# Attending the first batch in two halves of four heads

## The chip, the cores and the metric

One core of a Trainium2 chip runs the whole program. The metric is the device time of one execution in microseconds. Kernels that are compared ran alternately on the same chip. The kernel before took 986.52 us (median of 4 runs, 986.08 to 986.72).

## The reference, cut to what matters

```python
# attention, B, H, S, D = 8, 8, 576, 64
q_p, k_p = phi(q), phi(k)            # relu(x)*cos, relu(x)*sin, side by side: 128 features
kv  = einsum('bhsf,bhsd->bhfd', k_p, v);  z = k_p.sum(2)
num = einsum('bhsf,bhfd->bhsd', q_p, kv)
den = einsum('bhsf,bhf->bhs', q_p, z)[..., None] + 1e-6
x   = (num / den).transpose(0, 2, 1, 3).reshape(4608, 512)
# mixture of 8 experts, gates balanced by 8 rounds of row and column scaling over all tokens
out = sum_e P[:, e] * (relu(x @ w1[e]) @ w2[e])      # 512 -> 1024 -> 512
```

Each batch gives 576 tokens. The FFN walks through nine blocks of 512 tokens, so block 0 needs only batch 0, block 1 needs batches 0 and 1, and so on.

## The kernel before: the parts that matter

In this kernel TensorE (`te`), VectorE (`ve`) and ScalarE (`se`) each run their instructions in the order in which the program writes them: the helper below ties every call to the one before. A wait in one place therefore delays all that follows on that engine.

```python
class InOrder:                        # every call is tied to the one before on its engine
    def __getattr__(self, name):
        def call(*args, **kwargs):
            i = getattr(self.engine, name)(*args, **kwargs)
            not_before(self.last, i)
            ...

def keep_busy(n):                     # "fillers": products of ones, the result is not used
    for _ in range(n):
        te.matmul(out=idle_ps[:, 0:P], lhsT=ones_sq[:], rhs=ones_sq[:], start=True, stop=True)
```

The first batch is handled whole: queries, keys, values, sums, one set of denominators for all eight heads, with fillers in TensorE's waits. Then its four tiles of two heads each are attended; beside them the keys and values of batch 1 are prepared, and the first sixteen FFN products (four per tile) begin as soon as a tile is there.

```python
load(0, 0, "q"); ...; load(0, 1, "q")
for name in "kv": load(0, 0, name); load(0, 1, name)
...
for hk in range(HK):                  # q_p on VectorE, transposed on TensorE, moved by ScalarE
    prep_q(0, hk); ...turn(0, hk, i, True)
for hk in range(HK):
    prep_k(0, hk); prep_kp(0, hk)
keep_busy(16)
for half in range(2):
    prep_v(...); prep_v(...)
    begun.append(sums_begun(0, half))
    keep_busy((4, 6)[half])
sums_made(0, 0, begun[0]); sums_made(0, 1, begun[1])
epsilons(0)
denominators(0)                       # 24 products, then reciprocal, cast, remainder on VectorE
keep_busy(34)
...
for hk in range(HK):
    attend(0, hk)
    prep_k(1, hk); prep_kp(1, hk)     # keys of batch 1
    if hk >= 2: prep_v(1, hk - 2, se.copy)
    for kt in ((), (0,), (1,), (2, 3))[hk]:
        ...                           # four 512-wide FFN products for tile kt
```

The rest of batch 1 is placed into the 16 slots of block 0 (eight of the first FFN layer, eight half tiles of the second), and the start of batch 2 into its last slots:

```python
at(0, 4, prep_q, 1, 0); at(0, 4, ...sums_begun(1, 0)); at(0, 5, ...sums_made(1, 0)); ...
at(0, 8, denominators, 1)
at(0, 11 + hk, attend, 1, hk)
...
(11, prep_k, 0), (11, prep_q, 0), (12, prep_k, 1), (12, prep_kp, 0), ... # batch 2, block 0's slots
```

From batch 2 on the queries are transposed by a transfer, not by TensorE.

The softmax here doesn't subtract the row's maximum and nothing guards it: scores larger than these inputs give would overflow.

## Time and profile before

| | kernel before |
|---|---|
| time, us (median) | 986.52 |
| TensorE busy, share of the span | 98% |
| half clock after the start, us | 15.7 to 22.5 |
| first FFN product / last of the first sixteen ends, us | 25.1 / 30.5 |
| denominators of batch 1 end, us | 40.8 |
| block 1 starts / its gates start, us | 50.3 / 58.8 |

The page says where to look: after the start TensorE is nearly full. From 25 to 75 us it idles 1.6 us in all, from 75 to 175 us not at all, and its later waits (3.4 us between 175 and 225 us, some 6 us in the 760 us after that) are not touched by this change. Only the start can be won or lost. There the milestones of the last rows are read from the timeline of TensorE (first product of a kind, with its start). The prediction shows the lines.

### The profile page before, as it was taken

How to read it: one execution, taken by the hardware profiler on the slowest of the kernel's cores; microseconds unless marked ns; L12 is line 12 of the kernel's file. 1: busy time of each engine (PE TensorE's matmuls, PEld its weight loads, DVE VectorE, ACT ScalarE, POOL GpSimd, SP SyncE). 2: the span in 40 equal slices, each digit the busy share in tenths (PEclk: the TensorE clock that was granted, in tenths of full speed). 3: DMA queues.
4: the chain of work that ended last, by engine and by line, in shares of the span. 5: the costliest groups of instructions: out<-in, count | busy, mean ns of one | idle time of the engine just before them, and what ended most of it. 6: DMA issues, size and time to landing. Idle time of an engine off the chain costs nothing.

```text
span 984.8 us, 20226 instructions
## 1 busy us (share of the span) xinstructions
PE 969.9 (98%) x7844; PEld 678.4 (69%) x7844; DVE 805.8 (82%) x1830; ACT 568.6 (58%) x1269; POOL 60.6 (6%) x82
## 2 busy tenths in 40 slices
PE   8999999989999999999999999999999999999997
PEld 7545444447777777777777777777777777777775
DVE  5786774789889888988789888988888888988887
ACT  5776665467776555555555555555555555555551
POOL 6311110010000000000000000000000000000001
PEclk8999999999999999999999999999999999999999
DMA  9989990741013410133103400233103401104435
GB/s 162 206 122 162 157 151 9 136 77 47 34 41 68 85 32 25 49 68 68 49 25 69 91 25 25 56 62 67 49 25 68 92 25 27 47 26 117 128 87 129
DMA packets 80336, 73.54 MB, mean 75 GB/s; under 512 B 33264, under 2 KB 72176, under 8 KB 80240
## 3 DMA queue, kind: packets, MB, share of 16 engines
q0 software_dynamic: 27232, 30.94, 20.0%
q1 hardware_dynamic: 52768, 41.06, 17.2%
q8 instruction: 61, 1.00, 0.4%
q14 instruction: 35, 0.29, 0.1%
q10 hardware_dynamic: 240, 0.26, 0.1%
HBM read 83.12 MB, written 12.98 MB: 98 GB/s over the span
## 4 chain that ended last, share of the span: by engine, by line
PE 94%; DVE 2%; DMA 2%; ACT 1%; POOL 1%; issue 0%; POOLq 0%; ACTq 0%; SPq 0%
PE rows_ps L109 34%; PE h_ps L109 28%; PE copied_ps L109 11%; PE p_ps L109 11%; PE y_ps L109 6%; PE small_ps L109 4%; DMA v_ld<-in_v_dram 1%; DMA q_pT<-q_p 0%; DVE acc_hi L847 0%; POOL hs_last L862 0%; DVE P_tok L109 0%; DMA out_dram<-acc_lo 0%; DVE colp L109 0%; ACT u L109 0%; POOL k_ld L201 0%
## 5 line engine op out<-in xcount | busy, mean ns | idle before, releaser
L847 DVE SCALAR_TENSOR_TENSOR acc_lo<-rows_ps,P_tok,acc_lo 128x512 f32<-128x512 f32 (+1 forms) x322 | 203.1, 639 | 74.8 <-PE rows_ps L109 74.7
L109 PEld LDWEIGHTS <-H 128*128 128x128 f16 x2080 | 203.0, 98 | 83.1 <-issue 1.2
L783 ACT CAST u<-h_ps 128x384 f16<-128x384 f32 x288 | 137.6, 478 | 130.7 <-PE h_ps L109 130.7
L109 PEld LDWEIGHTS <-w1e 128*128 128x128 f16 x1632 | 156.4, 98 | 66.2 <-issue 6.0
L777 DVE CUSTOM_DVE_ANT_0 H<-p_ps,u 128x384 f16<-128x384 f32 x329 | 180.9, 550 | 6.7 <-PE p_ps L109 6.6
L109 PEld LDWEIGHTS <-hs 128*128 128x128 f16 x1500 | 146.6, 98 | 56.2
L109 PE MATMUL h_ps<-S,w1e 128*128 128x384 f16 x672 | 164.1, 326 | 1.1 <-ACT u L109 0.9
L109 PE MATMUL p_ps<-xT,T 128*128 128x384 f16 x672 | 164.1, 326 | 0.1
L109 PE MATMUL rows_ps<-V,H 128*128 128x256 f16 x1000 | 150.0, 273 | 0.7 <-DVE acc_hi L847 0.7
L109 PE MATMUL h_ps<-xT,w1e 128*128 128x384 f16 (+1 forms) x616 | 150.1, 350 | 0.2 <-DVE xT L109 0.2
L109 PE MATMUL rows_ps<-w2e,hs 128*128 128x256 f16 x1000 | 150.0, 273 | 0.0
L815 ACT ACTIVATE H<-h_ps 128x384 f16<-128x384 f32 x144 | 70.6, 490 | 95.1 <-PE h_ps L109 95.1
L109 PEld LDWEIGHTS <-T 128*128 128x128 f16 x1008 | 98.1, 98 | 29.5 <-issue 3.1
L109 PE MATMUL rows_ps<-w2e,H 128*128 128x256 f16 (+1 forms) x568 | 91.2, 285 | 0.0
L796 ACT COPY copied_ps<-h_ps 128x384 f32<-128x384 f32 x144 | 67.5, 469 | 36.0 <-PE h_ps L109 35.2
L806 ACT ACTIVATE H<-copied_ps 128x384 f16<-128x384 f32 x144 | 70.8, 492 | 20.4 <-PE copied_ps L109 20.4
L109 PE MATMUL h_ps<-S,T 128*128 128x384 f16 x336 | 81.8, 325 | 0.4 <-ACT copied_ps L109 0.3
L109 PE MATMUL copied_ps<-xT,w1e 128*128 128x384 f16 x336 | 82.1, 326 | 0.0
L109 PE MATMUL copied_ps<-w2e,H 128*128 128x256 f16 x504 | 75.5, 272 | 0.0
L109 PE MATMUL rows_ps<-V,hs 128*128 128x256 f16 x500 | 74.9, 272 | 0.0
L847 DVE SCALAR_TENSOR_TENSOR acc_lo<-copied_ps,P_tok,acc_lo 128x256 f32<-128x256 f32 x126 | 60.0, 476 | 0.4
L847 DVE SCALAR_TENSOR_TENSOR acc_hi<-rows_ps,P_tok,acc_hi 128x512 f32<-128x512 f32 (+1 forms) x56 | 41.3, 737 | 20.6 <-PE rows_ps L109 19.7
(140 smaller groups left out, 956.9 us busy)
## 6 DMA issues: line engine op xcount, KB each, us to landing
S<-x_saved SPq DMA_DIRECT2D x108, 192.0 KB, 2.4
out_dram<-acc_lo SPq DMA_DIRECT2D x62, 128.0 KB, 2.4
w1e<-in_moe_w_dram POOLq DMA_DIRECT2D x7, 1024.0 KB, 9.0
w2e<-in_moe_w_dram POOLq DMA_DIRECT2D x7, 1024.0 KB, 9.6
q_ld<-in_q_dram POOLq DMA_DIRECT2D x16, 288.0 KB, 7.4
k_ld<-in_k_dram POOLq DMA_DIRECT2D x16, 288.0 KB, 8.3
v_ld<-in_v_dram POOLq DMA_DIRECT2D x16, 288.0 KB, 9.4
x_saved<-S SPq DMA_DIRECT2D x18, 192.0 KB, 1.9
```

Of the source, the lines that this page charges most:

```text
L109: i = getattr(self.engine, name)(*args, **kwargs)
L777: latest = ve._custom_dve(TENSOR_ADD_SAT, out=out, in0=ps[:, 0:TU], in1=t[:], s0=FP32_MAX, s1=0.0)
L783: se.copy(out=t[:], in_=ps[:, 0:TU])
L796: se.copy(out=Y[:, 0:TU], in_=X[:, 0:TU])
L806: se.activation(out=h11, in_=Y[:, 0:TU], func=AF.Relu)
L815: se.activation(out=h12, in_=X[:, 0:TU], func=AF.Relu)
L847: ve.scalar_tensor_tensor(out=a, in0=rows, scalar=P_tok[:, g, self.e : self.e + 1], in1=a, op0=ALU.mult, op1=ALU.add,)
```

## The change

Its intent is to have the FFN products start sooner. The loads bring queries, keys and values of the first four heads ahead of the others. These heads get sums, denominators, a reciprocal chain (reciprocal, cast, remainder) and two attends of their own, so the first FFN products start while the other four heads still come in. The second half pays for its own denominators and reciprocals. In exchange, most fillers go (46 of the 60 between the parts of the batch), the weights of the first layer are loaded whole before batch 1, batch 1 is prepared later (slots 4 to 8 of block 0), batch 2 one slot later, and block 0's second layer first runs the half sums of all four tiles, two of them in PSUM tiles of the first layer.

```diff
-        load(0, 1, "q")
-        for name in "kv":
-            load(0, 0, name)
-            load(0, 1, name)
+        load(0, 0, "kv")
+        load(0, 1)
...
-        keep_busy(16)
-        for half in range(2):
-            prep_v(...)
-            begun.append(sums_begun(0, half))
-            keep_busy((4, 6)[half])
-        sums_made(0, 0, begun[0])
-        sums_made(0, 1, begun[1])
-        epsilons(0)
-        denominators(0)
-        keep_busy(34)
-        ... four attends, each with prep_k(1), prep_kp(1), prep_v(1) and FFN products
+        keep_busy(14)
+        ... prep_v(0, 0), prep_v(0, 1)
+        begin(0, 0)
+        epsilons(0)
+        made(0, 0)
+        prep_q(0, 2)
+        denominators(0, range(4))
+        turn_all(0, 2, True)
+        prep_k(0, 2)
+        prep_q(0, 3)
+        attend(0, 0)
+        prep_k(0, 3)
+        prep_v(0, 2, se.copy)
+        prep_kp(0, 2)
+        turn_all(0, 3)
+        prep_v(0, 3, se.copy)
+        attend(0, 1)
+        prep_kp(0, 3)
+        first(0)
+        begin(0, 1)
+        epsilons(0)
+        made(0, 1)
+        first(1)
+        denominators(0, range(4, 8))
+        attend(0, 2)
+        attend(0, 3)
+        first(2)
+        first(3)
...
+                for half in range(2):
+                    for hk in (2 * half, 2 * half + 1):
+                        at(0, 4 + half, prep_k, 1, hk, False)
+                        at(0, 4 + half, prep_kp, 1, hk)
+                        at(0, 4 + half, prep_v, 1, hk, se.copy)
+                at(0, 5, begin, 1, 0)
+                ... queries in slots 6 and 7, transposes in 7 and 8
-                    at(0, 11 + hk, attend, 1, hk)
+                    at(0, (10, 12, 13, 14)[hk], attend, 1, hk)
...
-                    (11, prep_k, 0), (11, prep_q, 0), (12, prep_k, 1), (12, prep_kp, 0), ...
+                    (12, prep_k, 0), (12, prep_q, 0), (13, prep_k, 1), (13, prep_kp, 0), ...
...
-                    if j == 0 and slot < FT + 4:
-                        ts, part = part, ts
+                    if j == 0:
+                        part, ts = divmod(slot - FT, TCH // P)
```

## The prediction

> **What bounds the kernel now.** I read the page first, then a table of stretches of the first 61 us, the timeline of TensorE, VectorE and ScalarE there, and the chain of work that ended last between 25 and 61 us.
>
> ```profile
> PE 969.9 (98%) x7844; PEld 678.4 (69%) x7844; DVE 805.8 (82%) x1830; ACT 568.6 (58%) x1269; POOL 60.6 (6%) x82
> PE 94%; DVE 2%; DMA 2%; ACT 1%; POOL 1%; issue 0%; POOLq 0%; ACTq 0%; SPq 0%
> ```
>
> TensorE is busy for 98% of the span and is 94% of the chain that ended last. The change touches only what happens before the second of nine token blocks (block 1) begins, so it can be worth only what TensorE loses there to waits, fillers and a low clock.
>
> ```profile
> 12.40:15.70 3.30, 1.05 (x41) 0.91 (x40) 2.38 (x5) 1.91 (x4) 1.54 (x3) 1.00 1.34 198
> 15.70:19.10 3.40, 3.40 (x61) 2.31 (x62) 0.73 (x5) 1.15 (x5) 2.08 (x3) 0.50 1.27 205
> 19.10:22.50 3.40, 3.40 (x44) 3.08 (x39) 2.08 (x3) 0.00 (x0) 1.43 (x2) 0.50 1.23 205
> 25.00:31.00 6.00, 5.80 (x36) 2.50 (x35) 5.82 (x12) 5.62 (x14) 2.85 (x4) 1.00 1.23 206
> 31.00:41.00 10.00, 9.08 (x153) 5.73 (x152) 6.05 (x15) 7.08 (x17) 5.15 (x8) 1.00 1.22 206
> 41.00:51.00 10.00, 10.00 (x76) 4.97 (x75) 7.95 (x18) 7.51 (x18) 0.56 (x1) 1.00 1.23 201
> ```
>
> Columns: stretch, length, busy time (and count) of PE, PEld, DVE, ACT, POOL, then granted clock, DMA share, GB/s. TensorE has 1.05 us of work between 12.4 and 15.7, and then runs at half clock until 22.5. Between 25 and 31 us VectorE (5.82 of 6) and ScalarE (5.62 of 6) are full: that is the attention of batch 0 with the keys of batch 1 prepared beside it. The transfers run at some 200 GB/s throughout.
>
> ```profile
> 14.60 1.03 PE L109 MATMUL small_ps<-acc_lo,k_p 64*128 64x65 f16 x36 [2.13 <-ACT acc_lo L109]
> 20.13 3.19 PE L109 MATMUL y_ps<-ones_sq 128*128 128x128 f16 x34
> 23.16 0.41 PE L109 MATMUL small_ps<-hl,acc_hi 96*128 96x192 f16 x3
> ```
>
> TensorE waited 2.13 us for values (all loads before them being first), then filled with 34 products of ones while VectorE made reciprocals. The first FFN product is at 25.1 us, the last of the sixteen "first" ones ends at 30.5.
>
> ```profile
> 34.04 0.23 DVE zsel L109
> 36.66 0.67 DVE q_p L109
> 37.33 0.93 DVE q_pT L109 x2
> 38.26 0.66 DVE q_p L109
> 39.39 1.00 DVE acc_hi L109 x2
> 40.76 0.97 PE y_ps L109 x4
> 50.50 1.74 PE h_ps L109 x8
> 54.39 4.09 DMA q_pT<-q_p
> ```
>
> This is the chain: after the first FFN products, the path is the preparation of batch 1 on VectorE and ScalarE up to its denominators (end 40.76); after that TensorE is dense and block 1 starts at 50.5. So two numbers decide: when the denominators of batch 1 are done, and what follows.
>
> [...] In the trace the loads land one after another, a 288 KB load per 1.43 us (counted from the packets), so a new order moves landings but not their sum.
>
> **The change part by part.**
>
> 1. Loads. Positions in the queue are served as seen by first users at 5.99, 8.45, 10.12, 13.03, 13.88 and 15.37 us. Before: both q, both k, both v halves. After: q, k, v of four heads, then of the others. The first values arrive at 10.12 instead of 13.88. w1 follows whole (about 16.7 to 20.6), then batch 1 (k, v by 26, q by 29), w2 by 34.5: none late for its user.
>
> 2. First half. VectorE: two q_p to 7.4, then two k (0.31+0.76 each) from 8.45 to 10.7. ScalarE: six transposed tiles to 10.4 (12 took 4.71 us before), two value copies (1.25) to 11.7. Sums end near 12.3 instead of 17.26. zsel (0.39), 12 denominator products: 13.1. But q_p of tile 2 stands in front of the reciprocal: 13.03 to 13.78. Then reciprocal 1.35, cast 0.31, hl 0.41: 15.9 instead of 22.4. Gain here 6.5 us.
>
> 3. Between the halves. attend(0) needs rb copies (0.70) and multiplications (0.82): 17.7. Then tile 3: relu of k (0.70), two value copies (0.66 each), k_p (0.76), two evictions on VectorE (0.55 each) and a third on ScalarE, all in front of attend(1), whose PSUM tiles come from the same four: xT 1 at 20.8, k_p 3 at 21.5, sums at 22.0.
>
> 4. Second half. It pays its own denominator: 23.6; a second VectorE chain of 1.35+0.31+0.41 = 2.07 us: 25.7. attend(2) 27.45, attend(3) 28.5, and the last first product 29.5, against 30.5. So of the 6.5 us only 1.0 is left: the second half comes through the same VectorE.
>
> 5. Clock. TensorE loses 46 of the 60 fillers between the batch's parts. Work of about 1.3 us from 12.4 to 15.7 is like the 1.05 of before, so I expect half clock from 15.7 here too, now under attend(0), tile 3 and the first FFN products. Half clock adds about 0.4 us to attend(0)'s two groups, 0.3 to attend(1), 0.4 in the sums: about 1.1 us, which takes the gain of 1.0.
>
> 6. Batch 1. Before, its relu, k_p and values were made in the full stretch from 25 to 31. After, they come behind it: VectorE does four relu (0.31) and four k_p (0.76), 28.5 to 32.8, and the four value copies stand between the evictions of hT on ScalarE: from 28.9 four hT 2.16, fifth 0.55, two values 1.25, hT 0.60, two values 1.25, kv_sb 0.43 gives 35.15; zsel 0.2 later: 35.35. Here VectorE was idle for two microseconds. Then on VectorE, in order: two q_p 1.5, eviction 0.55, zsel (behind kv_sb of the second half on ScalarE) 38.25, q_p 0.75, two evictions 1.0, q_p 0.75, three evictions 1.6: 42.35. Denominators of batch 1 end at 42.65, against 40.76.
>
> 7. From there to block 1 the work is that of before (seven half tiles of FFN2, the gates, four attends): 50.5 - 40.76 = 9.7 us. Taking all four first halves first lets attend(0) stand after the third half tile; its hl is ready 2.45 us after the denominators (0.35+1.35+0.30+0.41 and gaps), the work in front is 2.15: a stall of 0.3 at most.
>
> Sum: block 1 starts near 52.4 with full clock and 53.4 with half clock in between, instead of 50.5: +1.9 to +2.9 us. Afterwards TensorE is dense until 175 us, so the difference stays. A hand schedule with so many waits is good to perhaps 2.5 us, and the placing of the slots looks as if it had been tuned on the chip, which speaks for less; I take +1.5 us: 988.2.
>
> **Rivals.**
>
> A. The intended gain arrives: first FFN products at 20 us instead of 25.1, fillers of 3.19 us gone, and batch 1 catches up in the FFN slots because its loads have landed. For it: before, VectorE worked 30.9 of 45 us between 6 and 51, so there is room for the added 2.07. Against it: the room lies in waits of a serial chain. It would give 982.5 to 985.
>
> B. Half clock bites twice: [...]attend(2), attend(3) and eight large products (0.86 us more per four) run slow. +4 to +5 us: 991.
>
> C. Transfers hide everything: the landing of batch 2 sets block 1. Against: by packets batch 2 is in by 42 us, and the one wait in block 1 is 0.5 us, for a transpose that took 4.09 us while loads ran. If block 1 came 3 us earlier this wait would grow by perhaps 1 us and eat a third of A's gain. If it comes later, nothing changes.
>
> **Range and chances.** A at about 35% puts the time at 983 to 986.5, my schedule at 987.5 to 989.7 has about half, B the rest. The range is 984.3 to 991.3. Two per cent is 19.7 us, twice all that TensorE loses before block 1 (about 10 us from 14.6 on), so beyond 2% is nearly excluded: faster 0.01, same 0.98, slower 0.01.
>
> **What would show it.** Right: first hl near 16, second near 25.7; the last first product within a microsecond of 30; zsel of batch 1 waiting for kv_sb on ScalarE past 34.5; its denominators at 42 to 44; block 1 at 52 to 54; half clock from about 15.7[...]. Wrong: denominators of batch 1 before 40.7, or block 1 before 50; TensorE dense from 20 us on; full clock throughout. If block 1 starts earlier by some microseconds but the end doesn't follow, rival C was right.

## More of the kernel before

In the trace of the kernel before VectorE waits 2.84 us for the sums of batch 1, and the queries written after them start behind it, at 34.35 us.

## The result, and the profile after

The changed kernel took 995.69 us (median of 4 runs, 992.33 to 997.21) against 986.52. The ratio is 1.0089, with a 95% interval from 1.0062 to 1.0116; ratios are the mean time of one kernel's fast runs over that of the other's of the same rounds, so not quite the ratio of the medians. That is within 2%, as forecast, but 9.2 us slower and outside the predicted range. The runs also spread over 5 us, where those of before lie within 0.7 us. Their granted clocks sort them, but not all of the loss is in the mean clock: the run at 0.997, the mean clock of the kernel before in its profiled run, is still 5.8 us over.

```text
run      997.21  996.34  995.04  992.33 us
clock    0.990   0.990   0.991   0.997      (mean of the run)
```

The clock row of the page, 40 slices of 24.6 us before and 24.9 us after, shows a second dark slice. First before, then after:

```profile
PEclk8999999999999999999999999999999999999999
```

```profile
PEclk8899999999999999999999999999999999999999
...
PE 93%; DVE 3%; ACT 2%; DMA 1%; issue 0%; POOL 0%; ACTq 0%; SPq 0%; POOLq 0%
```

Here is the table of stretches after the change, in lengths of 3.4 us, cut where the clock changed. Half clock lasted 3.4, 6.8, 10.2, 13.7, 17.1 and 23.9 us in the profiled runs told of here, each close to a multiple of 3.4; one expectation below calls such a length a window. The columns are as in the prediction: after the busy times comes the granted clock.

```profile
12.50:15.90 3.40, 1.87 (x31) 1.12 (x28) 3.33 (x6) 2.46 (x7) 1.80 (x3) 1.00 1.37 198
15.90:19.30 3.40, 2.98 (x21) 1.75 (x18) 2.85 (x7) 3.16 (x8) 1.71 (x3) 0.50 1.43 199
19.30:22.70 3.40, 3.40 (x47) 1.55 (x46) 1.41 (x5) 0.43 (x2) 1.88 (x3) 0.50 1.21 206
22.70:26.20 3.50, 2.60 (x19) 0.84 (x16) 0.85 (x1) 0.00 (x0) 1.45 (x3) 0.50 1.21 207
26.20:29.60 3.40, 1.86 (x12) 0.80 (x13) 2.04 (x5) 0.80 (x3) 1.70 (x3) 0.50 1.22 205
29.60:33.00 3.40, 3.40 (x12) 1.28 (x12) 2.90 (x8) 0.91 (x3) 0.44 (x1) 0.50 1.24 206
33.00:36.40 3.40, 2.71 (x29) 1.24 (x28) 2.03 (x5) 3.40 (x8) 1.43 (x2) 1.00 1.21 206
```

Half clock lasted from 15.9 to 33.0 us: 17.1 us instead of 6.8. Under it lay the first sixteen FFN products, but for the end of the last, and the second half of the batch. The timeline shows what the intent was, that it arrived, and what it became:

```profile
18.95 1.03 PE L109 MATMUL h_ps<-xT,w1e 128*128 128x512 f16 x2
27.74 0.66 PE L109 MATMUL small_ps<-hl,acc_hi 96*128 96x192 f16 x3 [2.44 <-DVE hl L109]
32.87 0.66 PE L109 MATMUL y_ps<-xT,w1e 128*128 128x512 f16 x2
38.19 0.39 DVE L109 TENSOR_TENSOR zsel<-acc_hi,small_ps 128x64 f16<-128x64 f16 x2 [3.08 <-ACT kv_sb L109]
45.70 1.04 PE L109 MATMUL y_ps<-w2e,hT 128*128 128x512 f16 x4
66.10 0.34 PE L109 MATMUL small_ps<-q_pT,zsel 128*32 128x192 f16 x6 [1.42 <-DMA q_pT<-q_p]
66.89 3.37 PE L109 MATMUL h_ps<-xT,w1e 128*128 128x512 f16 x8
```

And the same waits in the kernel before (the first from its list of waits between 20 and 45 us: us in total, times, longest; the wait in question is the longest):

```profile
DVE zsel L109 <- ACT kv_sb L109: 3.5, 2, 2.8
58.52 0.35 PE L109 MATMUL small_ps<-q_pT,zsel 128*32 128x192 f16 x6 [0.52 <-DMA q_pT<-q_p]
59.31 1.89 PE L109 MATMUL h_ps<-xT,w1e 128*128 128x512 f16 x8
```

The first FFN product starts 6.2 us earlier than before. Then TensorE waits 2.44 us for the second reciprocal chain, and the last of the first sixteen ends at 33.5 us, 3.0 us later than before. VectorE sits idle for 3.08 us until ScalarE has moved the sums of batch 1; that wait was there before (2.84 us), but it now ends 4.2 us later. The denominators of batch 1 end at 45.8, 5.0 us later than before, and block 1 starts at 55.7. In block 1 there is a longer wait for a transpose, 1.42 us instead of 0.52, and after it eight products take 3.37 us instead of 1.89: the clock was lost once more, from 67.1 to 70.5 us. The gates of block 1 start at 66.4 (+7.6) and those of block 2 at 87.7 (+9.3). After that the kernels run alike, but for another 1.4 us by the end of this profiled run, the slowest of the four.

The chain of waits after the change has pieces that are new or longer (the piece of the transpose was 4.09 us before, that of the eight products 1.75):

```profile
25.35 1.36 DVE den L109
32.68 1.77 ACT hT L109 x4
35.64 0.72 ACT acc_lo L109
61.14 4.92 DMA q_pT<-q_p
67.03 3.23 PE h_ps L109 x8
```

The second reciprocal, the evictions of hT with the value copies of batch 1 among them, a transpose of batch 2, and slow products: each is a candidate, and the experiments take them one by one.

### The profile page after: what moved, and what is told of

Its sections match the earlier page's. It is cut to its first block, busy times and chain, and to the rows that moved or that the text cites.

```text
span 995.5 us, 20149 instructions
## 1 busy us (share of the span) xinstructions
PE 973.6 (98%) x7804; PEld 675.8 (68%) x7804; DVE 809.4 (81%) x1840; ACT 567.5 (57%) x1267; POOL 59.0 (6%) x80
## 4 chain that ended last, share of the span: by engine, by line
PE 93%; DVE 3%; ACT 2%; DMA 1%; issue 0%; POOL 0%; ACTq 0%; SPq 0%; POOLq 0%
PE rows_ps L109 33%; PE h_ps L109 28%; PE copied_ps L109 11%; PE p_ps L109 11%; PE y_ps L109 5%; PE small_ps L109 4%; ACT acc_lo L109 1%; DMA q_pT<-q_p 0%; DVE den L109 0%; ACT hT L109 0%; ACT q_pT L109 0%; DVE acc_hi L887 0%; ACT k_ld L109 0%; POOL hs_last L902 0%; DVE P_tok L109 0%
## 5 line engine op out<-in xcount | busy, mean ns | idle before, releaser
L109 PEld LDWEIGHTS <-w1e 128*128 128x128 f16 x1632 | 157.3, 98 | 69.6 <-issue 10.7
L109 PE MATMUL h_ps<-xT,w1e 128*128 128x384 f16 (+1 forms) x616 | 153.4, 356 | 0.3 <-DVE xT L109 0.3
L109 PEld LDWEIGHTS <-T 128*128 128x128 f16 x1008 | 98.1, 98 | 29.5 <-issue 3.1
## 6 DMA issues: line engine op xcount, KB each, us to landing
w2e<-in_moe_w_dram POOLq DMA_DIRECT2D x7, 1024.0 KB, 10.2
```

## The experiments

Three theories. **Clock**: the fillers that were taken out had kept the clock, and most of the loss is half clock. **Chain**: the order of work on VectorE and ScalarE (batch 1 late, values in front of evictions) makes the loss, and the clock only follows. **Slots**: what is lost inside block 1 comes from putting batch 2 one slot later. A fourth question came up on the way: what stands behind these.

"Over before" in the text is the median minus the median of the kernel before in the same rounds; it drifts by some tenths of a us from one set of rounds to another.

### Fillers put back, nothing else

```diff
-        keep_busy(14)
+        keep_busy(24)                      # before the values
...
         turn_all(0, 2, True)
+        keep_busy(20)                      # before attend(0)
...
         denominators(0, range(4, 8))
+        fill(30)                           # the same into a fresh PSUM tile: before attend(2)
```

> The changed kernel with products of ones put into the three waits of TensorE in the first batch: 24 instead of 14 before the values, 20 more before attend(0), 30 before attend(2); nothing else moves. Clock theory (the loss beyond 2 to 3 us is half clock, which came because the fillers were taken out): half clock falls from the 17 us of the changed kernel's profile to 7 us or none, no second half-clock stretch in block 1, first FFN products end near 30 us instead of 33.5, time 989 to 991.5 and runs within 1 us of each other. Chain theory (the loss is the order of work on VectorE and ScalarE, and the clock only follows): under 1.5 us gained, 994 to 996.

Measured: 989.22 us (988.23 to 989.98), ratio 1.0027 [1.0012, 1.0042]. 6.5 us of the 9.2 are gone. The same stretches with fillers:

```profile
19.30:22.70 3.40, 3.26 (x62) 1.50 (x59) 1.50 (x5) 0.43 (x2) 1.51 (x3) 1.00 1.22 207
22.70:26.20 3.50, 2.76 (x44) 2.18 (x39) 2.32 (x4) 0.60 (x2) 2.12 (x3) 1.00 1.21 206
26.20:29.60 3.40, 3.23 (x18) 1.42 (x18) 3.08 (x8) 1.88 (x6) 1.43 (x2) 1.00 1.23 206
```

The clock stays full until 38.6 us, and the first products end at 29.1 instead of 33.5. In the profiled run one stretch of 3.4 us was left, from 38.6 on, under the denominators of batch 1. The runs lie within 1.8 us, where the clock theory expected 1. It holds for the larger part. 2.7 us over before are left for the others.

### Which of the fillers

```diff
 a_fill1: keep_busy(24), keep_busy(20), no fill(30)
 a_fill2: keep_busy(14), no keep_busy(20), fill(30)
```

> The changed kernel with only the early fillers (24 before the values, 20 before attend(0)), none in the wait for the second reciprocal. If the early waits lose the clock and the dense products then hold it: close to the kernel with all fillers, 989 to 991, half clock at most one stretch of 3.4 us. If the wait of 2.4 us for the second reciprocal is enough to lose it by itself: half clock from about 26 us under the last eight first products, 991.5 to 994.

> The changed kernel with only the fillers in the wait for the second reciprocal. The clock is then lost at about 16 us as before, and the fillers bring it back one or two windows earlier than in the changed kernel (33 us): half clock 7 to 12 us, 990.5 to 993. If the early loss decides: 994 to 996, no gain.

Measured: 991.12 us (990.61 to 991.72) with the early ones alone, 992.54 us (990.17 to 992.9) with the late ones alone; over before 5.2 and 6.7. Neither is enough. In the profile with early fillers the clock is lost in the wait for the second reciprocal, without an earlier loss:

```profile
23.50:26.90 3.40, 1.37 (x12) 0.82 (x13) 2.38 (x5) 1.05 (x3) 1.87 (x3) 1.00 1.21 206
26.90:30.30 3.40, 3.40 (x11) 1.16 (x9) 3.03 (x8) 0.92 (x4) 1.71 (x3) 0.51 1.23 206
```

The first stretch has 1.37 us of work; after it comes half clock, under the last of the first products. With the late ones alone, half clock lasted from 13.7 to 27.4 us in the profiled run. So the change made two places in which the clock is lost, and the second one is new: it is the second reciprocal chain.

### The same fillers taken from the kernel before

```diff
-        keep_busy(16)
+        keep_busy(14)
...
-            keep_busy((4, 6)[half])
...
         denominators(0)
-        keep_busy(34)
```

> The kernel before with its fillers reduced to the 14 that the changed kernel keeps (16, 4, 6 and 34 become 14, 0, 0 and 0). Clock theory: the half-clock stretch lengthens from 6.8 us to 10 to 17 us and reaches the first FFN products, time 988.5 to 992, and the runs spread by more than 1 us. Chain theory: the fillers stood in waits anyway and nothing moves, 986 to 987.5.

Measured: 987.46 us (985.79 to 990.08), over before 0.9, ratio 1.0012 [0.9995, 1.003]: not clear of nothing, but with a spread of 4.3 us. The expectation of the clock theory was too high. In the profiled run half clock lasted 10.2 us, from 15.4 to 25.6, and the time was 985.79: no loss at all in that run. TensorE was busy for 7.8 of the 10.2 us, with sums, denominators and the first attends, and it waited 2.2 us for the reciprocal chain, but only the first four FFN products lay there; the first one started at 24.3, before the 25.1 of the kernel with fillers. There the 34 fillers, at half clock, end at 23.3 us, though the reciprocal chain is done at 22.4. So taking out fillers need not cost anything by itself. That half clock costs most where dense products and a serial chain lie under it, and that the change put both there, is a reading of these traces and was not tested apart.

### Batch 1 earlier in the changed kernel

```diff
         made(0, 1)
+        for hk in (0, 1): prep_k(1, hk); prep_kp(1, hk)
+        for hk in (0, 1): prep_v(1, hk, se.copy)
         first(1)
...      # and of the keys and values in slots 4 and 5 only the other two tiles' stay, in slot 5
-                at(0, 5, begin, 1, 0); at(0, 5, made, 1, 0)
+                at(0, 4, begin, 1, 0); at(0, 4, made, 1, 0)
```

> The changed kernel with keys and values of the first four heads of batch 1 prepared in the idle stretch of VectorE and ScalarE before the second reciprocal, and their sums one slot earlier. Chain theory: denominators of batch 1 end 2 to 3 us earlier than the 45.8 us of the changed kernel, block 1 starts 2 to 3 us earlier, time 992.5 to 994 with the half clock left as it is. Clock theory: the start of block 1 is set by the half-clock first products, under 1 us gained.

Measured: 996.08 us (995.43 to 996.5), no gain; the expectation of the chain theory failed. The denominators of batch 1 end at 45.9 us, as without the edit. VectorE now waited 5.1 us for the sums of batch 1 on ScalarE, then made the other two tiles' keys, and only then the queries. Half of the work was earlier, but the end of the line was not.

### Late batch 1 alone, in the kernel before

```diff
         for hk in range(HK):
             attend(0, hk)
-            prep_k(1, hk); prep_kp(1, hk); prep_v(...)
...
+ slots 4 to 8 of block 0 filled with batch 1 as in the changed kernel
```

> The kernel before with one part of the change alone: batch 1 prepared in slots 4 to 8 of block 0 as in the changed kernel, everything else and all fillers as before. The prediction's step 6 (late preparation costs 1.9 us): denominators of batch 1 near 42.5 us, 988 to 989.5. If VectorE and ScalarE, now unburdened during the attends, give it back: the first FFN products end 1 us or more earlier and the time is 986 to 987.5.

Measured: 988.37 us (988.27 to 989.78), ratio 1.003 [1.0018, 1.0043], over before 2.5. From the chain of waits of this kernel:

```profile
36.96 0.39 DVE zsel L109 x2
39.02 1.71 PE y_ps L109 x4
40.73 1.93 PE small_ps L109 x25
```

The denominators of batch 1 end at 42.66 us, 1.9 us later than before, though the first FFN products end at 29.0, 1.5 us earlier. The number is that of the prediction's step 6, but the late preparation is only a part of it. The second `zsel` pair, at 36.96 us, is 0.7 us later than before (36.27). The stretch before 38.6 us then has 2.05 us of TensorE work in 3.40, and from 38.6 to 42.0 us the clock is half once more: four products of the second layer take 1.71 us of the chain instead of 0.97. The remaining 1.2 us were lost there.

Two pairs of traces agree. The kernel with all fillers (`a_fill`) and the one with fillers and the old slots (`a_fill_slots`, below) are the same program up to slot 10 of block 0, and only the first has half clock from 38.6 to 42.0: its denominators end at 42.8 us, against 41.7. `a_fill_slots` and the first of the mended kernels (`a_best`, below) both keep the clock in their profiled runs and differ only in late or early preparation: 41.7 against 40.9 us, with medians 0.5 us apart and ranges that overlap. So late preparation by itself costs some 0.7 us at the denominators. What else lies in the 2.5 us was not separated.

### The order of the second layer alone, in the kernel before

```diff
-                    if j == 0 and slot < FT + 4:
-                        ts, part = part, ts
+                    if j == 0:
+                        part, ts = divmod(slot - FT, TCH // P)      # PSUM of two tiles from ps_h
...
-                    at(0, 11 + hk, attend, 1, hk)
+                    at(0, (10, 12, 13, 14)[hk], attend, 1, hk)
```

> The kernel before with one part of the change alone: block 0 runs the first halves of all four tiles up front, two of them in the PSUM tiles of the first FFN layer, with the attends of batch 1 at the changed slots. All theories say that this part is neutral: 986 to 987. If holding the PSUM tiles into block 1 costs something, 987.5 to 989.

Measured: 987.54 us (985.63 to 988.58), ratio 1.0012 [1.0, 1.0025]: at the edge of being clear, over before 1.6 by medians. In the trace attend(0) of batch 1 now comes before its reciprocal is there:

```profile
43.49 0.42 PE L109 MATMUL small_ps<-hl,acc_hi 96*128 96x192 f16 x3 [0.34 <-DVE hl L109]
```

and from the denominators of batch 1 to the gates of block 1 it takes 19.1 us instead of 18.0. The stall is 0.34 of that. For the rest, the trace shows ScalarE's rb copies and evictions bunched, so that PSUM comes free later; that is a reading of it, and the order and the slots of the attends were not tested apart. The part is not neutral, as I had expected; it costs about 1 us by the trace.

### The old slots for batch 2, without and with fillers

```diff
-                    (12, prep_k, 0), (12, prep_q, 0), (13, prep_k, 1), (13, prep_kp, 0), ...
+                    (11, prep_k, 0), (11, prep_q, 0), (12, prep_k, 1), (12, prep_kp, 0), ...
```

> The changed kernel with the preparation of batch 2 put back to the slots of before (11 to 15 instead of 12 to 15). If the late slots cause the loss inside block 1 (4 us there in the profile): the wait for the last transpose falls from 1.4 us to 0.5 or less, the half-clock stretch at 67 us goes, and the time falls by 2 to 4 us to 992 to 994. If the slots don't matter (VectorE is late for other reasons): within 1 us of the changed kernel.

> The changed kernel with both the fillers of the first experiment (989.2 us) and the old slots for batch 2 (993.3 us against 995.7). If the two losses are separate (half clock in the first batch; late slots in block 1), the gains add: 986 to 988. If the slots gained only by the clock (a half-clock stretch avoided in block 1), fillers have already taken that: 988.5 to 989.5.

Measured: 993.26 us (989.81 to 995.01) without fillers, a gain of 2.4; 987.89 us (987.64 to 988.9) with fillers, over before 2.0, a gain of 0.7 on 2.7. From the start of block 1 to its gates it took 7.8 us with the old slots, against 10.7 in the changed kernel, 9.6 in the one with fillers and 8.5 in the kernel before (block 1 itself starts later with the old slots, at 57.5, as half clock lasted 23.9 us in that profiled run). By the traces the late slots were a loss, most of it by the wait and the second half-clock stretch in block 1, and with the clock kept only a part of it is left. In the trace of the kernel with batch 1 earlier, the same late slots gave a wait of 1.39 us and no half clock after it, so that stretch does not come every time. The times alone don't settle it: the runs with old and with late slots overlap, in both pairs.

### Everything mended but the halves

```diff
 a_best:  fillers, old slots for batch 2, batch 1 as in the kernel before (keys and values
          beside the second half, queries from slot 4 on)
 a_best2: a_best, and the second layer's order and the attends' slots as in the kernel before
```

> The same, and batch 1 prepared and summed as in the kernel before: keys and values beside the second half of the first batch, queries from slot 4 on. If late preparation of batch 1 costs the 2 us that the prediction put on it: denominators of batch 1 end near 39.5 to 40 us, block 1 starts near 49.5, 984 to 985.5, that is faster than both kernels. If another wait takes its place (ScalarE's values before the evictions of hT): 986 to 988.

> The kernel that had fillers, early batch 1 and the old slots (987.4), with the second-layer order and the slots of the attends of batch 1 as before, so that of the change only the two halves of the first batch and the loads are left. By the trace of the kernel before with that part alone (stalls of 0.34 and about 0.5 us): 0.8 to 1.2 us gained, 986.0 to 986.6, that is equal to the kernel before within 0.5 us: the two halves bring nothing, since the denominators of batch 1 end no earlier. If the halves have a gain of their own: under 985.3.

Measured: 987.36 us (986.75 to 989.16), ratio 1.0018 [1.0005, 1.003], the second of the two outcomes expected; then 986.12 us (985.47 to 987.26), ratio 1.0006 [0.9994, 1.0018]. With the rest as before, the two halves with their loads and fillers bring nothing in the time and cost nothing clear of noise. Halves, loads and these fillers were not tested one without the other. The first FFN product is at 21.0 us in the profile of the latter, 4.1 us earlier than before, but the last of the sixteen ends at 31.6 (30.5 before) and the denominators of batch 1 at 41.8 (40.8 before). This is the slowest of its runs, with half clock from 14.8 to 18.2 us; in the profile of `a_best`, with full clock, the three are 19.5, 30.7 and 40.9. The start is earlier, but what ends the stretch is VectorE's and ScalarE's work for batches 0 and 1, and the halves add a second reciprocal chain to it (1.35 + 0.31 + 0.41 us in the kernel before).

### What lies behind: the kernel before with more fillers

```diff
-        keep_busy(16)
+        keep_busy(52)
```

> The kernel before with 52 instead of 16 fillers in its wait for the values. Clock theory carried to the kernel before: its one stretch of half clock from 15.7 to 22.5 us goes, sums and denominators run in full clock, first FFN product 1 to 1.5 us earlier than 25.1, 984.8 to 985.6. If VectorE and ScalarE bound the stretch after it: no gain, 985.8 to 986.5. If the fillers run over into the sums: 986.5 to 987.

Measured: 986.0 us (985.56 to 989.89), ratio 1.0017 [1.0002, 1.0032]. Four runs at clock 0.999 took 985.6 to 986.0, two at 0.996 took 989.6 and 989.9. In the profiled run the half clock is gone up to the end of the span; the first FFN product starts at 22.7 and the denominators of batch 1 end at 38.3, 2.5 us earlier than before. So with full clock on both sides the kernel without halves is 2.6 us ahead at this point (38.3 against the 40.9 of `a_best`). The time is that of the second outcome expected, but not for its reason: the stretch did get faster. All but 0.5 us is given back in block 1:

```profile
53.79 0.76 DVE L109 TENSOR_TENSOR q_p<-q_ld,acc_hi 128x1152 f16<-128x1152 f16 x1 [2.73 <-DMA q_pT<-q_p]
55.27 0.46 PE L109 MATMUL small_ps<-acc_lo,k_p 64*128 64x65 f16 x18 [2.59 <-DVE k_p L109]
```

VectorE waits for a q_p buffer that a transpose is still reading (the run with four buffers, below, no longer has this wait). Times from issue to landing of the transposes up to about 80 us (the traces' queries of the tile they write, 40 to 80 us), first of the kernel before and then of this one:

```profile
DMA to landing us min/median/max: 3.2/4.5/6.3
```

```profile
DMA to landing us min/median/max: 3.2/3.8/9.3
```

In the kernel before the transfers run at some 200 GB/s until 50 us (206 from 48 to 50), and a load takes 10.8 us from issue to landing (the median of the q loads). In the kernel with 52 fillers a load was issued at 41.65 us, and a transpose of batch 2 issued at 44.4 landed at 53.7.

### Trying to lift that wait

First, the loads of batch 3 held back to the start of block 1:

```diff
-                    at(1, 0, load, b + 2, half)
+                    at(1, 0, load, b + 2, half, "qkv", True)
```

> The kernel before with the loads of batch 3 held back to the start of block 1. If the transposes of batch 2 are slowed by these loads: their time to landing falls from 4 to 5 us to about 3.3, the wait of 0.5 us in block 1 goes, 985.2 to 985.7. If batch 3 now comes too late for block 1: new waits, 986.5 to 989.

> The kernel before with 52 fillers and the loads of batch 3 held back. If the transposes behind the loads are the floor that ate the 2.5 us of the run with 52 fillers: no transpose over 5 us, gates of block 1 at about 56 us instead of 58.3, 982.8 to 984 in runs that keep the clock. If another floor stands there (batch 3 late, VectorE): 985 to 986.5.

> The mended changed kernel (986.1) with the loads of batch 3 held back. Its denominators of batch 1 end at 41.8 us, no earlier than in the kernel before, so if VectorE and ScalarE eat the gain of the halves in the first batch, nothing is hidden behind the transposes: 985.6 to 986.3. If the floor of the transposes hid a gain: under 985.2.

Measured: 1001.52 us (999.18 to 1002.69), 998.63 us (998.22 to 999.75) and 1001.64 us (1000.38 to 1002.99): 12 to 15 us slower, and none of my expectations. The six loads were now issued in one burst just when the last transposes of batch 2 were. In the first of the three:

```profile
DMA to landing us min/median/max: 3.2/3.3/14.9
```

One transpose took 14.9 us, TensorE waited 11.1 us in two places, and half clock came on top: eight products from 70.5 us on took 3.34 us instead of 1.90. The experiment did not lift the wait. It shows the same from the other side: 3.2 us for the quickest transpose of this trace, and 14.9 us for the slowest, beside the burst of loads.

Then a fourth q_p buffer, with one of rb's four given up:

```diff
-        qp_pool = ... bufs=3; ... rb_pool = ... bufs=4
+        qp_pool = ... bufs=4; ... rb_pool = ... bufs=3
```

> The kernel before with four q_p and three rb buffers. It has no wait for a q_p buffer, so nothing should move: 985.6 to 986.8.

> The kernel before with 52 fillers, four q_p and three rb buffers. If the q_p buffer behind the slow transpose was the wait that ate the gain: no wait of VectorE for a transpose, gates of block 1 at 56 to 57 us instead of 58.3, 983.8 to 985.2 in runs that keep the clock. If the denominators of batch 2 then wait for the transpose itself: gates at 57.5 to 58.5, 985.3 to 986.3.

> The mended changed kernel with four q_p and three rb buffers: it has no wait for a q_p buffer either, so 985.5 to 986.6; under 985 would mean that the halves had a gain that the buffer hid.

Measured: 986.37 us (985.43 to 986.77), 986.92 us (984.82 to 988.85) and 985.71 us (985.11 to 987.34), with ratios 1.0, 1.0008 and 1.0001 and intervals that hold 1. In the second, the wait of VectorE is gone, and TensorE waits for the transposes themselves:

```profile
PE small_ps L109 <- DMA q_pT<-q_p: 2.3, 3, 1.2
```

The gates of block 1 start at 57.8 us, against 58.3 with three buffers and 58.8 in the kernel before. For the gates that was the second of the two outcomes expected; the time lies above it. In this profiled run the clock was lost behind the waits, from 58.8 to 62.2 us, and the gates of block 2 start at 79.2, later than the 78.4 of the kernel before. So a start earlier by 2 to 3 us reaches block 1's gates as 0.5 to 1 us, because TensorE waits 2.3 us for the transposes of batch 2 (with three buffers one of them took 9.3 us from issue to landing), and in this profiled run 3.4 us of half clock followed. No version beat the kernel before beyond the noise.

## Why the prediction was wrong

The direction was right, and so was the place: half clock from about 15.7 us and late denominators of batch 1. The size was not: 988.2 us forecast with a range up to 991.3, 995.69 measured.

- **Step 5 failed.** It said that half clock "adds about 0.4 us to attend(0)'s two groups, 0.3 to attend(1), 0.4 in the sums: about 1.1 us". That assumed a stretch as long as before, 6.8 us. It lasted 17.1 us in the profile, plus 3.4 in block 1, and putting fillers back won 6.5 us: 4.4 of them are there when the first FFN products end (29.1 us against 33.5). The step counted the fillers taken out and did not ask how long half clock would last without them. The wait for the second reciprocal, which step 4 had written down itself, was a second place to lose it.
- **Rival B named this** ("half clock bites twice") but as an extra 2 us on top of the sum, with the smallest weight. Even its 991 was too low, as the slow clock also lay under the second half's sums and denominators and came once more in block 1.
- **Steps 2 to 4 hold where the clock holds.** With fillers back, the first products end at 29.1 us (forecast 29.5).
- **Step 6 has the right path and twice its size.** With the clock full (fillers and old slots), the denominators of batch 1 end at 41.7 us, 0.9 later than before; the forecasts were 42.65 and 1.9. With fillers alone they end at 42.8, and block 1 starts at 52.7 (forecast 52.4); both are near the forecast by luck, as 1.2 us of half clock lie in them. The same holds for the 1.9 us of late batch 1 in the kernel before. The step also passed over that VectorE waits for these sums in the kernel before too (2.84 us).
- **Step 7 was right.** From the denominators of batch 1 to block 1 the changed kernel takes 9.9 us, with a stall of 0.33 us; the forecasts were 9.7 and 0.3 at most.
- **"The difference stays"**: this was wrong too. Between the start of block 1 and the gates of block 2 some 4 us were added, by a later batch 2, a wait of 1.42 us for a transpose, and 3.4 us of half clock after it. The later slots of batch 2 have no step in the prediction.
- **Rival C was underrated.** It expected the wait to grow by 1 us if block 1 came 3 us earlier. In the kernel before with 52 fillers block 1 came 2.5 us earlier and 2.6 us of waiting took it back.

Of the prediction's own signs, half clock came where it said (15.9 us) and `zsel` waited for ScalarE until 38.2 us. The denominators of batch 1 (45.8) and block 1 (55.7) lie past its 42 to 44 and 52 to 54.

What stays open: which of the halves, the loads and the fillers makes the mended kernel (`a_best`) 2.6 us later at the denominators of batch 1 than the kernel before with 52 fillers; and why full clock follows one stretch in which TensorE is busy for all of 3.40 us and not another (last section). The parts also don't add up to the last half microsecond, since the sets of rounds differ by that much.

## What to carry to other kernels

Before taking out products that only fill waits, ask what will keep the clock in their place, stretch by stretch, and what dense work lies behind each new wait: here putting fillers back won 6.5 of the 9.2 us, and a wait of 1.42 us was followed by eight products that took 1.5 us longer. Starting the bound engine's work sooner is worth nothing if the stretch ends by another engine's queue; read which wait ends last before and after, and then the next one behind it (here transposes, up to 9.3 us from issue to landing). When a forecast number comes true, check that its cause did: 1.9 us of late preparation were 0.7 us of it and 1.2 us of half clock. When runs of one kernel spread more than those of another, sort them by granted clock before anything else: with 52 fillers, four runs at 0.999 took 985.6 to 986.0 us and two at 0.996 took 989.6 and 989.9.

## What the traces show of the clock and of the transposes

- The clock was lost after a stretch of 3.40 us with 1.87 us of work whose longest gap was 1.33 us (changed kernel, half clock from 15.9 us), and after one of 3.40 us with 1.37 us of work with early fillers alone (half clock from 26.9 us). It was lost after as much as 2.45 us of work in 3.40 (the mended kernel with a fourth buffer, half clock from 18.2 us) and kept after 2.30 (the changed kernel, 9.1 to 12.5 us), so busy time alone does not say when.
- Full clock did not follow every stretch that the trace shows busy for all of its 3.40 us. Half clock went on after 15.7 to 19.1 us in the kernel before and after 19.3 to 22.7 us in the changed one; it ended after 19.1 to 22.5 us in the first and after 29.6 to 33.0 us in the second. The two after which it went on hold products with few rows or columns (64 rows, 1 row, 32 columns); whether that matters was not tested.
- Transposes of 128 x 1152 two-byte elements took 3.2 us from issue to landing at the quickest, up to 9.3 us with 52 fillers, where a load had been issued 2.7 us earlier, and 14.9 us beside a burst of six loads (loads of batch 3 held back in the kernel before).
